# Top-k attention with a Fourier mix: the first batch's top-k mask computed on GpSimd alone

## Chip, cores and metric

The kernel runs on one core of a Trainium2 chip. The metric is the device time of one execution in microseconds (us). The engines are named as in the profile: PE (TensorE, matrix products and transposes) with PEld (its weight loads), DVE (VectorE), ACT (ScalarE), POOL (GpSimd) and SP (SyncE, which issues the DMAs).

## What is computed

The inputs are q, k and v of 8 batches, 8 heads, 576 tokens and 64 dimensions, and two weights of 512 x 2048 and 2048 x 512. Everything is float32 inside the kernel; the weights can come as float64 words and are then converted on the chip.

```python
scores = scale * np.matmul(q, k.transpose(0, 1, 3, 2))
kth = np.partition(scores, -32, axis=-1)[..., -32:-31]
scores = np.where(scores >= kth, scores, -1000000000.0)
scores = scores - np.max(scores, axis=-1, keepdims=True)
attn = np.exp(scores)
attn = attn / (np.sum(attn, axis=-1, keepdims=True) + 1e-09)
x = np.matmul(attn, v)               # then heads side by side: 8 x 576 x 512
mixed = np.real(np.fft.fft(np.fft.fft(x, axis=1), axis=2))
u = x + mixed
un = (u - mean(u)) / np.sqrt(var(u) + 1e-06)
out = u + np.maximum(un @ w_ch1, 0.0) @ w_ch2
```

Of each row of 576 scores, the 32 largest are kept and the rest are given a weight of zero by the exponential. The Fourier transforms are done as products with tables of cosines and sines.

## The kernel before

**Tiles and steps.** The attention is cut into 288 tiles of 128 rows and 576 scores (`items`): two heads at a time (a pair), nine tiles for each pair, four pairs and so 36 tiles (`PER_BATCH`) for each batch. One loop with the index `i` runs over the tiles, and one pass of it is a step. The order in which each engine gets its instructions is the order in which this loop emits them: the schedule is written out by hand, engines work through their queues in that order, and semaphores hold an instruction until its inputs are there. Some work is put into a plan with a step and a place in the step (`at(step, where, fn)`), and the loop fetches it there.

**What a tile needs.** `scores` multiplies on PE and copies the result on ACT into a buffer `S` in the on-chip memory (lines L335, L353, L364). `top_ops` finds the 32 largest values on DVE in four rounds: MAX8 (L382) gives the eight largest of a row, and MATCH_REPLACE8 (L384) takes them out in a work buffer `wk`. The four groups of eight are in `M8`. `bounds` (L391) multiplies the first and the last of these 32 by -1 and by the constant `FAR` (2^100) on POOL, into `nt`. `mask` then makes, on ACT, the value relu(-FAR * s + FAR * m32) in `wk` (L398), which is zero where the score is kept and huge elsewhere, and subtracts it on POOL from the score (L399). `expo` (L405) takes the exponential on ACT, and sums the row. `transposes` turns the result on PE (L426, L437, L441), ACT copies it out (L429, L438, L442, L444), and `attend` multiplies with v (L463). `to_tokens` transposes the outcome back (L503), and DVE divides by the sums (L490, L507, L514).

**First batch and later ones.** In the first batch the chain is short: in step i, `bounds(i)` and `mask(i)` are emitted at the end of the step, and `expo(i-1)` and `transposes(i-1)` in the middle of it. From tile 36 on, `mask(i-1)` is emitted one step later, and the transposes two steps later. In the first batch there is also the conversion of the weights, one block of 128 x 512 in nearly every step from step 1 to 33: three operations on ACT (L186, L202, L205) at the beginning of the step, one on DVE (L193), and two on POOL (L212 and L213) after the mask's subtraction. Two stages of matmuls with a matrix of equal entries (L1202) give the means of a part of the weights in steps 19 and 27, ACT copies these out (L1215), and POOL subtracts them (L1211) in eight of the first batch's steps; the other half follows after the first batch.

**After the first batch.** Once its 36 tiles are done, DVE folds the token axis and the channel axis of the result (L601, L564, L548 and the copies L552 and L560), POOL folds the few rows left over, PE does the transform over tokens (`yp`, L633) and over channels (`mp`, L681), DVE adds these to x and takes the statistics (L687, L709, L710), PE transposes (L746), and the first multiplications of the two-layer block begin (L831). From here on the matmuls of that block for one batch are spread in `units` over the attention of the next.

The buffers that matter: six for `S`, three pairs for `wk`, five for `M8`, six for `nt`.

Of the kernel before, what the change touches and what calls it, by code (L numbers as in the profile page):

```python
# [12 lines left out]
AF = mybir.ActivationFunctionType  # L13
ALU = mybir.AluOpType

TOPK = 32
NEG = -3.4028234e38
FAR = 2.0 ** 100
# [46 lines left out]
def kernel(  # L65
# [9 lines left out]
    nc = tc.nc  # L75
# [3 lines left out]
    scale = 1.0 / float(D) ** 0.5  # L79
# [57 lines left out]
    cc = const.tile([P, 2], F32, name="cc", tag="cc")  # L137
# [80 lines left out]
    nat, qT_of, kT_of, v_of, PT, Ssb, Wk, Wp, M8, Nt = ({} for _ in range(10))  # L218
# [76 lines left out]
    PER_BATCH = NPB * PER_PAIR  # L295
# [91 lines left out]
    def bounds(i):  # L387

        if i < N:
            Nt[i] = small.tile([P, 2], F32, name=f"nt_{i}", tag="nt", bufs=6)  # L390
            nc.gpsimd.tensor_tensor(  # L391
                out=Nt[i], in0=M8.pop(i)[:, 0:TOPK:TOPK - 1], in1=cc, op=ALU.mult
            )

    def mask(i):

        w = Wk[i]
        nc.scalar.activation(out=w, in_=Ssb[i], func=AF.Relu, scale=-FAR, bias=Nt[i][:, 1:2])  # L398
        nc.gpsimd.tensor_tensor(out=w, in0=Ssb.pop(i), in1=w, op=ALU.subtract)  # L399

    def expo(i):
# [834 lines left out]
    for o, place in ((B12, w2_12), (B21, w2_21)):  # L1236
        at(PER_BATCH + 14, "load2", lambda o=o, place=place: nc.sync.dma_start(
            out=scr[:, o], in_=place
# [106 lines left out]
    i, carry = 0, 0.0  # L1345
    while i < N + 4 or plan or queue or sums:
# [58 lines left out]
        for n, fn in enumerate(fixed):  # L1405
            cost += fn()
            if n == n_mask:
                if PER_BATCH <= i - 1 < N:
                    mask(i - 1)
                run(i, "act")  # L1410
                for fn in out_next:
                    fn()
                out_next.clear()
            if n == min(n_tr, len(fixed) - 1) and PER_BATCH <= i - 1 < N:
                expo(i - 1)

            got += some(max(room * (n + 1) / len(fixed) - got, 1.1 if fn in preps else 0.0))
# [29 lines left out]
        run(i, "pool0")  # L1447
        some_sums(max(2.1 - planned, 0.0))
        bounds(i)

        some_sums(1.3)
        if i < PER_BATCH:
            mask(i)
# [45 lines left out]
```

## Time and profile before

| | |
|---|---|
| time, median of 3 runs | 1915.32 us (1914.49 to 1915.92) |
| profiled execution: span from the first to the last instruction | 1910.9 us |
| profiled execution: its own time | not listed apart; the three runs lie 3.6 to 5.0 us above the span |
| PE busy | 1802.4 us (94% of the span) |
| DVE busy | 1584.9 us (83%) |
| ACT busy | 1208.4 us (63%) |
| POOL busy | 870.5 us (46%) |
| relu L398 on ACT | 288 times, 788 ns |
| mask subtraction L399 on POOL | 288 times, 1416 ns |
| bounds L391 on POOL | 288 times, 192 ns |
| exponential L405 on ACT | 288 times, 780 ns |
| MAX8 L382 on DVE | 1152 times, 743 to 749 ns |
| join of the weights, L212 and L213 on POOL | 32 times each, 1288 and 1290 ns |

Busy time is the time in which an engine works on an instruction. A line such as L398 is a line of the kernel, and all of its executions are one group. In the timeline, each row has the start in us from the beginning of the span, the duration in us, the engine, the line, the operation, output<-input with their shapes, and how many instructions are merged into the row; in brackets stands how long the engine was idle before, and what ended that. In a list of waits, "A <- B: t, n, m" says that the engine of A was idle before A until B ended, t us in all, n times, and m us the longest. The granted clock is the share of TensorE's full speed that it was given.

### The profile page before, as it was taken

Reading aid. Unit: us, or ns where it says so; the run is one execution under the profiler, and the core shown is the slowest. Engines: PE = TensorE matmul, PEld = TensorE weight load, DVE = VectorE, ACT = ScalarE, POOL = GpSimd, SP = SyncE. Lnnn points to the kernel's source line nnn. Section 1 sums busy time; section 2 is a strip of 40 time slices with the busy share of each in tenths; the row PEclk is TensorE's granted clock in tenths of the full one; section 3 lists DMA queues with packets and bytes.
Section 4 is the critical chain, followed back from the end, with each engine's and each line's share of the span. In section 5 each row is a group of like instructions: output and inputs, shape, how many; then the busy total and the mean of one; then the engine's idle time right before and its main releaser. Section 6 shows DMA issues by size and latency. Waiting matters only on the chain.

```text
span 1910.9 us, 28281 instructions
## 1 busy us (share of the span) xinstructions
PE 1802.4 (94%) x9008; PEld 1195.1 (63%) x9008; DVE 1584.9 (83%) x3277; ACT 1208.4 (63%) x3078; POOL 870.5 (46%) x1158
## 2 busy tenths in 40 slices
PE   6666699999999999999999999999999999999999
PEld 3344475474666756766567656667567656767678
DVE  8999989999999998989899898888899988872110
ACT  6878657676766767666676667666676667652110
POOL 4768643545635364345535454345534454241022
PEclk8777799999999999999999999999999999999999
DMA  5333001321104111140013101140013102030132
GB/s 164 105 96 107 20 13 45 93 66 25 47 11 129 29 28 44 42 121 19 20 47 101 53 16 53 42 114 23 22 47 101 49 20 58 23 102 6 50 100 79
DMA packets 184339, 111.34 MB, mean 58 GB/s; under 512 B 125952, under 2 KB 174208, under 8 KB 184192
## 3 DMA queue, kind: packets, MB, share of 16 engines
q1 hardware_dynamic: 183408, 109.33, 20.0%
q8 instruction: 72, 1.18, 0.3%
q14 instruction: 75, 0.61, 0.1%
q10 hardware_dynamic: 784, 0.21, 0.1%
HBM read 93.76 MB, written 15.73 MB: 57 GB/s over the span
## 4 chain that ended last, share of the span: by engine, by line
PE 80%; POOL 8%; ACT 4%; issue 3%; DVE 2%; DMA 1%; SPq 0%; POOLq 0%; ACTq 0%; DVEq 0%
PE hp L831 25%; PE cp L858 10%; PE o L463 8%; PE sp L361 6%; PE tpP L426 5%; PE cw L1028 5%; PE cv L1028 4%; PE yp L633 3%; PE mp L681 3%; POOL wk L399 3%; PE cp L897 3%; POOL w L213 2%; POOL w L212 2%; PE sp_t L331 2%; DVE m L382 1%
## 5 line engine op out<-in xcount | busy, mean ns | idle before, releaser
L399 POOL TENSOR_TENSOR wk<-S,wk 128x576 f32<-128x576 f32 x288 | 407.8, 1416 | 797.8 <-ACT wk L398 768.9
L382 DVE MAX8 m<-wk 128x8 f32<-128x576 f32 x864 | 623.3, 749 | 5.3
L831 PE MATMUL hp<-unT,w 128*128 128x256 f32 (+1 forms) x2048 | 536.7, 409 | 2.6 <-ACT unT L749 2.6
L831 PEld LDWEIGHTS hp<-unT,w 128*128 128x128 f32 x2048 | 372.7, 190 | 123.5 <-issue 23.8
L384 DVE MATCH_REPLACE8 wk<-m,wk 128x576 f32<-128x576 f32 x576 | 427.6, 742 | 0.0
L405 ACT ACTIVATE wk<-wk,nt 128x576 f32<-128x576 f32 x288 | 224.7, 780 | 68.1 <-POOL wk L399 64.1
L426 PE MATMUL tpP<-ident,wk 128*128 128x128 f32 x1152 | 185.8, 286 | 70.5 <-ACT wk L405 45.1
L429 ACT COPY PT<-tpP 128x512 f32<-128x512 f32 (+1 forms) x320 | 171.1, 546 | 113.5 <-PE tpP L426 111.1
L398 ACT ACTIVATE wk<-S,nt 128x576 f32<-128x576 f32 x288 | 226.9, 788 | 22.6 <-POOL nt L391 21.5
L858 PE MATMUL cp<-w,hT 128*128 128x512 f32 x512 | 240.6, 598 | 0.0
L426 PEld LDWEIGHTS tpP<-ident,wk 128*128 128x128 f32 x1152 | 142.6, 146 | 144.3 <-ACT wk L405 66.4
L835 ACT ACTIVATE hT<-hp 128x320 f32<-128x320 f32 (+1 forms) x256 | 104.8, 409 | 192.7 <-PE hp L831 190.4
L382 DVE MAX8 m<-S 128x8 f32<-128x576 f32 x288 | 214.0, 743 | 8.2 <-ACT S L335 8.2
L384 DVE MATCH_REPLACE8 wk<-m,S 128x576 f32<-128x576 f32 x288 | 213.6, 742 | 0.0
L463 PE MATMUL o<-PT,v 128*64 128x256 f32 (+3 forms) x1440 | 193.8, 412 | 1.4 <-ACT PT L429 1.4
L364 ACT COPY S<-sp 128x512 f32<-128x512 f32 (+1 forms) x264 | 141.7, 588 | 54.2 <-PE sp L361 54.1
L361 PE MATMUL sp<-kT,qT 64*128 64x512 f32 (+1 forms) x528 | 162.0, 672 | 4.2 <-ACT means L1215 3.3
L463 PEld LDWEIGHTS o<-PT,v 128*64 128x64 f32 x1440 | 111.3, 152 | 72.5 <-issue 16.2
L858 PEld LDWEIGHTS cp<-w,hT 128*128 128x128 f32 x512 | 88.8, 190 | 86.3 <-issue 86.2
L973 POOL TENSOR_TENSOR hT<-hT 128x512 f32<-128x512 f32 x64 | 81.3, 1274 | 100.4 <-ACT hT L835 88.7
L1028 PE MATMUL cw<-w,hT 128*128 128x256 f32 x448 | 106.4, 383 | 1.4 <-POOL nt L391 1.2
L1028 PEld LDWEIGHTS cw<-w,hT 128*128 128x128 f32 x448 | 81.5, 190 | 18.6 <-issue 5.2
(143 smaller groups left out, 2147.5 us busy)
## 6 DMA issues: line engine op xcount, KB each, us to landing
w<-w_parts SPq DMA_DIRECT2D x82, 512.0 KB, 4.3
space<-in_moe_w_ch_dram SPq DMA_DIRECT2D x32, 512.0 KB, 3.3
nat<-in_q_dram SPq DMA_DIRECT2D x128, 64.0 KB, 2.2
v<-in_v_dram SPq DMA_DIRECT2D x128, 64.0 KB, 2.2
out_dram<-x SPq DMA_DIRECT2D x32, 256.0 KB, 2.1
nat<-in_k_dram SPq DMA_DIRECT2D x124, 64.0 KB, 2.1
w_parts<-w_t SPq DMA_DIRECT2D x8, 512.0 KB, 2.9
w_s<-w_parts SPq DMA_DIRECT2D x8, 512.0 KB, 4.8
```

The lines of the kernel that those rows point to most:

```text
L361: nc.tensor.matmul(sp[r], lhsT=qT[hd, q_cols], rhs=kT[hd, :], start=True, stop=True)
L382: ops.append(lambda src=src, m8=m8: nc.vector.max(out=m8, in_=src))
L384: ops.append(lambda src=src, m8=m8: nc.vector.match_replace(w, m8, src, NEG))
L398: nc.scalar.activation(out=w, in_=Ssb[i], func=AF.Relu, scale=-FAR, bias=Nt[i][:, 1:2])
L399: nc.gpsimd.tensor_tensor(out=w, in0=Ssb.pop(i), in1=w, op=ALU.subtract)
L405: nc.scalar.activation(out=w, in_=w, func=AF.Exp, bias=Nt.pop(i)[:, 0:1], accum_out=den_t[pair % 3][:, c:c + 1],)
L426: nc.tensor.transpose(tp[:, c, :], p_sb[:, k0 + P * c:k0 + P * (c + 1)], ident)
L429: nc.scalar.copy(out=pt[:, NF * he:NF * (he + 1), col:col + w], in_=tp[:, :, o:o + w])
L463: nc.tensor.matmul(o[D * e:D * (e + 1), c0:c1], lhsT=vv[:, c, e, :], rhs=pt[:, 2 * NF if c == NF else NF * e + c, c0:c1], start=(c == 0), ...
L831: nc.tensor.matmul(hp[:, 0:w], lhsT=w1[:, dt, P * it:P * (it + 1)], rhs=unT[:, dt, 0:w], start=(dt == 0), stop=(dt == NDT - 1),)
L858: nc.tensor.matmul(cp, lhsT=hT[:, it, P * n:P * (n + 1)], rhs=w2[:, it, :], start=(it == 0), stop=(it == NIT - 1),)
L1028: nc.tensor.matmul(dst, lhsT=h()[a][:, kc, :], rhs=rhs_of(kc), start=start and kc == 0, stop=kc == NK - 1, skip_group_check=True,)
```

## The change

For the 36 tiles of the first batch, the mask's first half is done on POOL instead of ACT: one `tensor_scalar` compares each score with the 32nd maximum of its row (1 where it is less, 0 elsewhere) and multiplies by `FAR`. The subtraction on POOL stays as it was. `bounds` is still computed, since the exponential uses its first column; its second column isn't used in the first batch any more. `M8` is now released by the comparison and not by `bounds`. From tile 36 on nothing is changed.

```diff
         if i < N:
             Nt[i] = small.tile([P, 2], F32, name=f"nt_{i}", tag="nt", bufs=6)
+            m8 = M8[i] if i < PER_BATCH else M8.pop(i)
             nc.gpsimd.tensor_tensor(
-                out=Nt[i], in0=M8.pop(i)[:, 0:TOPK:TOPK - 1], in1=cc, op=ALU.mult
+                out=Nt[i], in0=m8[:, 0:TOPK:TOPK - 1], in1=cc, op=ALU.mult
             )
 
     def mask(i):
 
         w = Wk[i]
-        nc.scalar.activation(out=w, in_=Ssb[i], func=AF.Relu, scale=-FAR, bias=Nt[i][:, 1:2])
+        if i < PER_BATCH:
+            nc.gpsimd.tensor_scalar(
+                out=w, in0=Ssb[i], scalar1=M8.pop(i)[:, TOPK - 1:TOPK], scalar2=FAR,
+                op0=ALU.is_lt, op1=ALU.mult,
+            )
+        else:
+            nc.scalar.activation(
+                out=w, in_=Ssb[i], func=AF.Relu, scale=-FAR, bias=Nt[i][:, 1:2]
+            )
         nc.gpsimd.tensor_tensor(out=w, in0=Ssb.pop(i), in1=w, op=ALU.subtract)
```

## Prediction

> **What bounds the kernel now.** I read the table of busy time by stages first, then who waited for whom, then single steps in the timeline. In the first table the columns are length of the stretch, busy us and instructions of PE, PEld, DVE, ACT and POOL, granted clock, DMA share and GB/s:
>
> ```profile
> 16.00:130.00 114.00, 73.30 (x354) 46.76 (x353) 112.90 (x231) 93.30 (x217) 73.73 (x74) 0.78 0.38 121
> 130.00:220.00 90.00, 56.78 (x286) 36.38 (x286) 85.74 (x175) 71.82 (x168) 72.33 (x70) 0.74 0.25 75
> 262.00:1911.00 1649.00, 1624.37 (x8150) 1083.03 (x8148) 1341.59 (x2772) 1017.89 (x2628) 712.24 (x980) 1.00 0.19 53
> ```
>
> Two regimes are to be seen. From 262 us on PE is busy for 1624 of 1649 us, so whatever moves the moment at which PE enters that stretch moves the end by the same amount. Before it, in the 36 tiles of the first batch, DVE is the full engine (112.9 of 114 us; 85.7 of 90), with its top-32 search. The edit lies wholly in that first stretch, and takes work off ACT (93 of 114 us), which is not full. The waits up to 240 us (of DVE; sum, times, longest) and up to 280 us (of POOL) say who holds whom:
>
> ```profile
> DVE m L382 <- ACT S L335: 3.0, 5, 0.7
> DVE w L193 <- ACT wh L186: 0.7, 2, 0.4
> ```
>
> ```profile
> POOL wk L399 <- ACT wk L398: 63.9, 39, 5.2
> ```
>
> DVE hardly waits; what it does wait for is ACT's copies of later scores. POOL waits before nearly every mask subtraction for the relu on ACT. One undisturbed POOL round, from the timeline:
>
> ```profile
> 34.36 0.20 POOL L391 TENSOR_TENSOR nt<-m,cc 128x2 f32<-128x2 f32 x1
> 35.44 1.42 POOL L399 TENSOR_TENSOR wk<-S,wk 128x576 f32<-128x576 f32 x1 [0.89 <-ACT wk L398]
> 36.81 1.29 POOL L212 TENSOR_TENSOR w<-w,space 128x512 int32<-128x512 int32 x1
> 38.18 1.29 POOL L213 TENSOR_TENSOR w<-w,space 128x512 f32<-128x512 f32 x1
> 39.42 0.20 POOL L391 TENSOR_TENSOR nt<-m,cc 128x2 f32<-128x2 f32 x1
> ```
>
> A round is 5.06 us, 1.08 of them from the bounds to the subtraction with 0.89 idle. Eight rounds (tiles 20-23 and 28-31) also carry a weight centring (L1211) and take 6.28 us (140.58 to 146.86), while DVE's ordinary step is 5.55 us. So POOL, with ACT in its ring, falls behind: tile 20's maxima are ready at 129.2 and its bounds start at 133.55; for tile 32 the lag is 6.5 us. Behind POOL come ACT's exp and copies, and it is then that DVE runs dry: its idle times before 227 us are 0.44, 0.70, 0.70, 0.70, 0.56 and 0.34, together 3.44 us, all after 147 us. The last tile of the batch, 35:
>
> ```profile
> 219.99 0.19 POOL L391 TENSOR_TENSOR nt<-m,cc 128x2 f32<-128x2 f32 x1
> 223.31 0.80 ACT L398 ACTIVATE wk<-S,nt 128x576 f32<-128x576 f32 x1
> 224.19 1.41 POOL L399 TENSOR_TENSOR wk<-S,wk 128x576 f32<-128x576 f32 x1 [4.01 <-ACT wk L398]
> 225.63 0.78 ACT L405 ACTIVATE wk<-wk,nt 128x576 f32<-128x576 f32 x1 [1.52 <-POOL wk L399]
> 230.36 0.44 PE L503 MATMUL tpx<-ident,xT 128*128 128x128 f32 x2 [0.46 <-ACT xT L477]
> 231.00 0.17 DVE L490 RECIPROCAL rd<-rd 128x4 f32<-128x4 f32 x1
> 240.94 1.36 DVE L560 COPY fsp<-fsp 128x2 f32<-128x2 f32 x1
> 247.53 3.62 PE L681 MATMUL mp<-fd,y 128*128 128x256 f32 x16
> ```
>
> Its bounds are ready at 220.2, but ACT reaches the relu, behind its copies, only at 223.31. DVE's folds follow (to 242.3), the token DFT's second half runs 243.5 to 247.5, the channel DFT starts at 247.53, and PE's full stretch begins.
>
> **What the Trainium skill says.** The GPSIMD Engine Reference, section 4.1 Engine selection, calls one-input work on GpSimd roughly line rate and two-input work about twice as slow; its section 3.1 gives 1.03 cycles an element for a small body, about 1.8 for a good loop, about 2.6 with two inputs, and 12 with data-dependent branching. The trace agrees for two inputs: 128x576 in 1416 ns against 128x512 in 1274 ns is 2.2 ns an element. No wide one-input operation of POOL but a memset (128x513 in 520 ns) is in the trace. Perfetto Trace Analysis, section GPSIMD Engine Instruction, advises timing POOL by start-to-start spacing; I do so (1.24 us after an L213 shown as 1.29). SBUF — State Buffer, section Who interferes with whom, says that a DVE operation with two SBUF inputs, or in a two-port mode, and a GpSimd one block each other. One fold copy of DVE agrees: 1.24 us at 234.40 beside a mask subtraction, 0.17 at 239.53.
>
> **The change, part by part.** *Removed:* 36 relus of 0.78 us, 28 us of ACT, each of them a wait in ACT's queue for POOL's bounds, with the next step's three weight conversions (L186, L202, L205), exp and score copies queued behind it. ACT was not full, so the 28 us are worth only what they release. *Added:* 36 tensor_scalar operations of 128x576 on POOL, of a time T that the trace does not show. From below, a line-rate pass costs 0.19 (the shortest operations) + 576 x 0.82 ns (the memset's slope) = 0.66 us; the 1.8-cycle loop gives 0.19 + 0.86 = 1.05; as slow as the two-input form it would be 1.42; with branching, 5.9. I take 0.85, between the first two, as one input and two arithmetic steps. No DMA moves, and the last maxima's buffer is freed one instruction later, with five buffers: nothing.
>
> *POOL's round after.* Bounds to tensor_scalar 0.15 (the spacing after an L391), then T, 0.08 to a dependent operation (as from L212 to L213), then 3.98 as before: 4.22 + T, and 5.44 + T with centring. At T = 0.85 that is 5.07 and 6.29, what the unheld rounds are now. The work replaces the wait one for one; the gain is that holds longer than 0.89 us, 20 us in the 36 tiles, go. Tile 19 alone is held 5.2 us and starts the lag. Without that, tiles 20 to 32 cost POOL 8 x (5.44 + T) + 5 x (4.22 + T) = 64.6 + 13T, and DVE 77.7 - 2.5 of idle = 75.1: a lag at tile 33 of 13T - 10.5 = 0.6 us in place of 5.0.
>
> *What that is worth.* ACT and PE, no longer behind POOL, have the scores ready, and DVE's 3.44 us go. The folds then end at 242.3 - 3.4 = 238.9; PE, whose chain from tile 35 starts some 4 us earlier (subtraction about 1.1 us after the maxima, now 5.2), is waiting; the second half of the token DFT takes 4.0 us, and the channel DFT starts near 243.0 in place of 247.5: 4.5 us at most, apart from another 1 us if the fold copy is not blocked. If DVE keeps its waits, the same sum gives 246.4, a gain of 1.1. I take 4.3. The span goes from 1910.9 to 1906.6; about 4.4 us lie between the profiled span and the median of 1915.32, so the forecast is **1911.0**.
>
> **Rivals.** *Half of it, or nothing (0.22).* DVE's waits come from PE's long stages (the mean matmuls, 3.6 us in one piece, sit between scores and transposes) and not from POOL, or T is 1.1 to 1.45: between -3.5 and +3.5 us, near 1914. For it speaks that ACT's relu 19 waited not for POOL but for ACT's own queue behind those matmuls, which stay; against it, that every DVE wait falls in the stretch where POOL lags. That the relu's removal frees nothing because exp still needs POOL's subtraction belongs here.
>
> *POOL becomes the bound (0.28).* The mechanism is T alone, in POOL's queue from tile 20 on. The lag at tile 33 is 13T - 10.5; it changes by T - 1.45 to tile 34 (5.67 us of DVE) and by T - 4.26 to tile 35 (no joins), so tile 35's subtraction starts 16T - 16.0 us after its maxima, against 5.2 now. It decides from T = 1.33. At T = 1.65, with about 1 us carried from earlier tiles, that is +6 us: 1921.5. At 1.8, with 3.5 us carried, +11: 1926. Lateness here goes to the end undiminished, for DVE takes up tile 35's tokens at 231.00, 0.2 us after they are transposed. For it speaks that a comparison has to be turned into a number and multiplied, a longer body than any POOL runs here; against it, the single input.
>
> **How the numbers follow.** A difference within 0.2% (3.8 us) is about what a measurement of this kernel can tell from no change. The likeliest case straddles that line, 3.8 to 6 us faster with a chance of 0.50, its own range being 1909 to 1911.5; the middle case has 0.22, slower 0.28. The range runs from 1908.5 (all DVE waits and the blocked copy gone, and a little more) to 1922 (T about 1.65); left out are slower T, some 0.15, and a few hundredths below.
>
> **What would show it.** Right: tensor_scalar near 0.85 us; no L398 before 220 us; POOL's longest idle before L399 in tiles 1 to 35 near zero; tile 32's bounds within 3 us of its maxima; DVE without waits for S up to 227 us; the channel DFT starting near 243; PE's sum after it unchanged. Wrong: tensor_scalar above 1.3 us, with bounds ever further behind the maxima; or the waits of DVE for S still there with POOL on time, which would put them down to PE's stages.

## The result and the profile after

The changed kernel takes 1943.83 us (median of 4 runs, 1941.98 to 1947.8) against 1914.95 us of the kernel before (median of 4, those of the table and one more): 28.9 us slower, ratio 1.0151 with a 95% interval from 1.0137 to 1.0166. The profiled execution has a span of 1940.2 us, 29.3 more than before, and its own time is 1941.98, so 1.8 us lie around the span. The forecast of 1911.0 with a range to 1922 was wrong, and on the wrong side.

Busy time by stages of the kernel after, with the columns explained in the prediction:

```profile
16.00:130.00 114.00, 60.53 (x306) 38.89 (x306) 104.27 (x211) 71.27 (x172) 107.78 (x86) 0.70 0.37 115
130.00:220.00 90.00, 54.56 (x258) 32.95 (x258) 74.78 (x151) 56.12 (x135) 86.87 (x70) 0.73 0.25 76
300.00:1940.00 1640.00, 1614.65 (x8104) 1076.53 (x8102) 1334.26 (x2758) 1012.48 (x2616) 704.41 (x968) 1.00 0.19 54
```

POOL, the fifth engine, has gone from 73.7 to 107.8 us of 114 and from 72.3 to 86.9 of 90: it is now the full one. DVE has fallen from 112.9 to 104.3 and from 85.7 to 74.8. PE's long stretch is what it was, with 25 us idle. One POOL round in the timeline of the kernel after (L392 is the bounds, L400 the comparison, L408 the mask's subtraction):

```profile
41.55 0.20 POOL L392 TENSOR_TENSOR nt<-m,cc 128x2 f32<-128x2 f32 x1
41.83 2.21 POOL L400 TENSOR_SCALAR wk<-S,m 128x576 f32<-128x576 f32 x1
44.12 1.40 POOL L408 TENSOR_TENSOR wk<-S,wk 128x576 f32<-128x576 f32 x1
45.48 1.29 POOL L212 TENSOR_TENSOR w<-w,space 128x512 int32<-128x512 int32 x1
46.84 1.29 POOL L213 TENSOR_TENSOR w<-w,space 128x512 f32<-128x512 f32 x1
48.09 0.19 POOL L392 TENSOR_TENSOR nt<-m,cc 128x2 f32<-128x2 f32 x1
```

No row shows an idle bracket: POOL works without a pause, 6.54 us a round where the one of before took 5.06 with its wait. The comparison takes 2.21 us where 0.85 was assumed, and all 36 of them take 2.21 or 2.22. Who waits for POOL is seen in the list of waits of ACT from 16 to 255 us and of DVE to 255 us, kernel after:

```profile
ACT wk L414 <- POOL wk L408: 73.3, 32, 6.3
```

```profile
DVE m L382 <- ACT S L335: 28.7, 14, 4.1
DVE x L516 <- PE tpx L512: 1.3, 1, 1.3
DVE w L193 <- ACT wh L186: 0.7, 2, 0.5
```

ACT's exp (L414) waits for POOL's subtraction 32 times, 73.3 us in all. ACT's copies of later scores stand behind exp in its queue, and so DVE waits 28.7 us for scores where it waited 3.0. The longest of these waits, in the timeline:

```profile
228.27 0.78 ACT L414 ACTIVATE wk<-wk,nt 128x576 f32<-128x576 f32 x1 [3.27 <-POOL wk L408]
229.05 0.30 ACT L335 COPY S<-sp_t 128x64 f32<-128x64 f32 x2
229.34 0.76 DVE L382 MAX8 m<-S 128x8 f32<-128x576 f32 x1 [4.08 <-ACT S L335]
```

All three lines of DVE's list together are 30.7 us, against 3.7 before: 27.0 us more, and that is the loss but for 0.8 us at the channel transform. It passes unchanged through the rest: the channel transform of the first batch starts 27.8 us later (247.53 before), and so does that of the second batch.

```profile
275.29 3.62 PE L690 MATMUL mp<-fd,y 128*128 128x256 f32 x16
```

### The profile page after: what moved, and what is told of

It is laid out like the page before. It is cut to its first block, busy times and chain, and to the rows that moved or that the text cites. A ratio compares the mean times of both kernels' runs of the same rounds, so it can differ in the third digit from the quotient of the medians.

```text
span 1940.2 us, 28332 instructions
## 1 busy us (share of the span) xinstructions
PE 1800.9 (93%) x9008; PEld 1194.7 (62%) x9008; DVE 1584.5 (82%) x3277; ACT 1186.0 (61%) x3042; POOL 949.1 (49%) x1194
## 4 chain that ended last, share of the span: by engine, by line
PE 79%; POOL 7%; DVE 6%; ACT 4%; issue 2%; DMA 2%; SPq 0%; POOLq 0%; DVEq 0%; ACTq 0%
PE hp L840 25%; PE cp L867 10%; PE o L472 7%; PE sp L361 6%; PE tpP L435 5%; PE cw L1037 5%; PE cv L1037 4%; PE yp L642 3%; PE mp L690 3%; PE cp L906 3%; DVE m L382 3%; DVE wk L384 2%; POOL wk L400 2%; POOL wk L408 2%; PE sp_t L331 2%
## 5 line engine op out<-in xcount | busy, mean ns | idle before, releaser
L408 POOL TENSOR_TENSOR wk<-S,wk 128x576 f32<-128x576 f32 x288 | 406.9, 1413 | 749.8 <-ACT wk L405 717.9
L414 ACT ACTIVATE wk<-wk,nt 128x576 f32<-128x576 f32 x288 | 225.1, 781 | 135.4 <-POOL wk L408 131.3
L405 ACT ACTIVATE wk<-S,nt 128x576 f32<-128x576 f32 x252 | 198.9, 789 | 11.5 <-POOL nt L392 10.6
L1037 PEld LDWEIGHTS cw<-w,hT 128*128 128x128 f32 x448 | 81.5, 190 | 19.4 <-issue 5.2
```

What stands on the lines that cost most here:

```text
L414: nc.scalar.activation(out=w, in_=w, func=AF.Exp, bias=Nt.pop(i)[:, 0:1], accum_out=den_t[pair % 3][:, c:c + 1],)
L1037: nc.tensor.matmul(dst, lhsT=h()[a][:, kc, :], rhs=rhs_of(kc), start=start and kc == 0, stop=kc == NK - 1, skip_group_check=True,)
```

## The experiments

### Which part of the operation costs 2.2 us

The first batch's comparison was replaced by twelve forms in turn; this is the core of the edit:

```diff
-            nc.gpsimd.tensor_scalar(
-                out=w, in0=Ssb[i], scalar1=M8.pop(i)[:, TOPK - 1:TOPK], scalar2=FAR,
-                op0=ALU.is_lt, op1=ALU.mult,
-            )
+            form(i % 12, w, Ssb[i], M8.pop(i)[:, TOPK - 1:TOPK])
...
+        if n == 0:
+            ts(out=o, in0=s, scalar1=m32, scalar2=FAR, op0=ALU.is_lt, op1=ALU.mult)
...
+        elif n == 5:
+            ts(out=o, in0=s, scalar1=0.5, scalar2=1.0, op0=ALU.mult, op1=ALU.add)
+        elif n == 6:
+            ts(out=o, in0=s, scalar1=0.5, scalar2=None, op0=ALU.mult)
...
```

> The 36 masks of the first batch use twelve forms of the one-input operation on POOL in turn, three tiles each, all 128x576 (two forms as two halves of 288); the mask itself is therefore not computed in 33 of them. If the comparison is what is slow: forms with is_lt 2.2 us, forms with subtract, mult, add, min or max at most 1.1 us. If the second arithmetic step is: one-step forms about 1.1 us, two-step forms 2.2 us. If the per-partition scalar is: forms with it 2.2, with two immediates at most 1.1 us. If tensor_scalar on POOL as such is slow: all near 2.2 us, the copy alone near 0.7. If the time is per element and not per instruction, a half takes 1.2 us; if it is a fixed cost, a half takes over 1.8 us.

From the groups by line and shape of this kernel (after the bar: busy us in all, mean ns of one). L399 is is_lt and mult, L405 subtract and min, L401 is_lt alone, L411 mult alone with an immediate, L409 mult and add, L421 the copy, L415 and L419 the halves of L399 and L409:

```profile
L415 POOL TENSOR_SCALAR wk<-S,m 128x288 f32<-128x288 f32 x6 | 7.5, 1255 | 0.5
L405 POOL TENSOR_SCALAR wk<-S,m 128x576 f32<-128x576 f32 x3 | 6.7, 2223 | 0.0
L399 POOL TENSOR_SCALAR wk<-S,m 128x576 f32<-128x576 f32 x3 | 6.7, 2223 | 0.3
L401 POOL TENSOR_SCALAR wk<-S,m 128x576 f32<-128x576 f32 x3 | 5.2, 1733 | 0.0
L411 POOL TENSOR_SCALAR wk<-S 128x576 f32<-128x576 f32 x3 | 5.0, 1661 | 0.0
L419 POOL TENSOR_SCALAR wk<-S 128x288 f32<-128x288 f32 x6 | 2.5, 436 | 0.0
L409 POOL TENSOR_SCALAR wk<-S 128x576 f32<-128x576 f32 x3 | 2.0, 679 | 0.0
L421 POOL COPY wk<-S 128x576 f32<-128x576 f32 x3 | 2.0, 666 | 0.0
```

None of the four causes that were expected is right by itself. It isn't the comparison: subtract and min take as long, and a single multiplication takes 1.66 us, more than twice the pair of mult and add. That the time is per element, and not a fixed cost, came true: a half takes 1.26 us, and 576 columns against 288 give 3.4 ns an element for is_lt and mult, and 0.84 for mult and add. A second step costs 0.5 us in the dear forms, a scalar for each partition 0.08.

Twelve more forms were run to find where the cheap kind ends:

```diff
+        if n == 0:
+            ts(out=o, in0=s, scalar1=0.5, scalar2=0.5, op0=ALU.mult, op1=ALU.add)
...
+        elif n == 3:
+            ts(out=o, in0=s, scalar1=m32, scalar2=m32, op0=ALU.mult, op1=ALU.add)
+        elif n == 4:
+            ts(out=o, in0=s, scalar1=0.5, scalar2=m32, op0=ALU.mult, op1=ALU.subtract)
+        elif n == 5:
+            ts(out=o, in0=s, scalar1=0.5, scalar2=0.5, op0=ALU.add, op1=ALU.mult)
...
```

> Twelve more forms of the one-input operation of 128x576 on POOL, three tiles each in the first batch, whose mask is left out by that. If the fast time of 0.68 us belongs to mult followed by add: mult and add with a scalar for each partition, also 0.7 us; all others 1.65 to 2.25 us, also mult and mult, add and mult, max and min. If it belongs to two immediates without comparison: mult and mult, add and mult, max and min, subtract and mult with immediates 0.7 us, those with a partition's scalar 1.7 to 2.25 us.

The groups of this kernel: L399 is mult and add with immediates, L405 the same with two scalars for each partition, L411 mult and mult, L409 add and mult, L407 mult and subtract, L421 subtract and mult with immediates, L413 max and min:

```profile
L407 POOL TENSOR_SCALAR wk<-S,m 128x576 f32<-128x576 f32 x3 | 6.7, 2222 | 0.0
L421 POOL TENSOR_SCALAR wk<-S 128x576 f32<-128x576 f32 x3 | 6.4, 2147 | 0.0
L413 POOL TENSOR_SCALAR wk<-S 128x576 f32<-128x576 f32 x3 | 6.4, 2141 | 0.0
L405 POOL TENSOR_SCALAR wk<-S,m 128x576 f32<-128x576 f32 x3 | 2.5, 818 | 0.0
L399 POOL TENSOR_SCALAR wk<-S 128x576 f32<-128x576 f32 x3 | 2.0, 673 | 0.0
L411 POOL TENSOR_SCALAR wk<-S 128x576 f32<-128x576 f32 x3 | 2.0, 671 | 0.0
L409 POOL TENSOR_SCALAR wk<-S 128x576 f32<-128x576 f32 x3 | 2.0, 671 | 0.0
```

Neither expectation is right in full: the scalars for each partition are cheap with mult and add, as the first said, but mult and mult and add and mult are cheap as well, and max and min is not, against the second. In the 20 different forms tried, the cheap ones are exactly those of two steps that are both mult or add, 0.67 to 0.82 us whatever the operands (add followed by add was not tried). Every other one takes 1.65 to 2.22 us. The copy is cheap, too. Why the others are dear is not shown.

### Was the rest of the sum right? T turned to 0.68 and to 1.73 us

Two kernels differ from the changed one in the form alone:

```diff
-                out=w, in0=Ssb[i], scalar1=M8.pop(i)[:, TOPK - 1:TOPK], scalar2=FAR,
-                op0=ALU.is_lt, op1=ALU.mult,
+                out=w, in0=Ssb[i], scalar1=0.5, scalar2=1.0, op0=ALU.mult, op1=ALU.add
```

> As the changed kernel, but the one-input operation in the first batch is mult by 0.5 and add 1.0, the form that took 0.68 us; the mask of the first batch is left out by that, the work of all other instructions stays. Theory 1 (the step that failed was T alone, the rest of the prediction's sum holds): POOL's round is 5.0 us without and 6.2 us with centring, bounds start within 2 us of the maxima for tile 32, DVE's waits for scores before 227 us are gone, the channel DFT starts near 243 us, and the time is 3.5 to 5 us below before: ratio 0.9974 to 0.9982. Rival (DVE's waits come from PE's and ACT's long stages): POOL is on time and the waits stay; the gain is 1 us or less, ratio 0.9993 to 1.0003.

Measured: 1910.01 against 1914.9 us, ratio 0.9976 (0.9965 to 0.9987), 4.9 us faster. DVE's waits up to 230 us in this kernel are those of the first scores and of the start alone:

```profile
DVE S L335 <- PE sp_t L331: 8.1, 1, 8.1
DVE cc L1136 <- PEq L1488: 0.8, 1, 0.8
```

The channel transform starts 7.8 us earlier than before:

```profile
239.71 3.62 PE L690 MATMUL mp<-fd,y 128*128 128x256 f32 x16
```

Tile 32's bounds start 1.7 us after its maxima (6.5 before), and a round with centring takes 6.1 us. So POOL, freed of its wait for the relu, does take DVE's waits with it. With the mask left out, exp gets other values; it takes 0.78 us here, as in the kernels before and after.

```diff
-                out=w, in0=Ssb[i], scalar1=M8.pop(i)[:, TOPK - 1:TOPK], scalar2=FAR,
-                op0=ALU.is_lt, op1=ALU.mult,
+                out=w, in0=Ssb[i], scalar1=M8.pop(i)[:, TOPK - 1:TOPK], scalar2=None,
+                op0=ALU.is_lt,
```

> As the changed kernel, but with the comparison alone, without the multiplication by the constant: T is 1.73 us in place of 2.21, and the mask of the first batch is left out. Theory 1 (a queue with a threshold: only what POOL's round has above DVE's step of 5.66 us adds up): round 6.06 us, 0.40 above; the sum of the prediction gives 11.7 us behind the maxima at tile 35, some 4.2 carried from the tiles before 20 and 1.8 for the dearer start of the operation, less 5.2 now: 10 to 14 us slower than before, ratio 1.005 to 1.0075. Rival (the loss is in proportion to POOL's added work): 28.9 x 1.73 / 2.21 = 22.6 us slower, ratio 1.0118.

Measured: 1924.98 against 1914.9 us, ratio 1.0055 (1.0041 to 1.0069), 10.1 us slower, at the low end of what the queue with a threshold gives and less than half of what proportion would. Three points, at T = 0.68, 1.73 and 2.21, give -4.9, +10.1 and +28.9 us: from 1.73 to 2.21 the cost is 18.8 us for 36 x 0.48 = 17.3 us of added work, one for one within the intervals; from 0.68 to 1.73 it is 15.0 us for 37.8 us of work. Below the threshold added work goes into POOL's idle time, and above it everything counts. POOL's round in this kernel is 5.95 us (6.06 were expected). An estimate from such rounds says where the threshold lies: without the operation, POOL's 34 rounds from tile 1 to 35 are 148 us, and DVE's 34 steps without waits took 193 in the kernel with the fast form, so the two meet at T = 45 / 34 = 1.3 us. From there 34 times the excess is 14 us at T = 1.73 and 31 at 2.21; measured against the kernel with the fast form, it is 15.0 and 33.8.

### Was the relu's time on ACT worth anything?

First the relu was kept, and the comparison done beside it:

```diff
         nc.scalar.activation(out=w, in_=Ssb[i], func=AF.Relu, scale=-FAR, bias=Nt[i][:, 1:2])
+        m8 = M8.pop(i)
+        if i < PER_BATCH:
+            nc.gpsimd.tensor_scalar(
+                out=extra, in0=Ssb[i], scalar1=m8[:, TOPK - 1:TOPK], scalar2=FAR,
+                op0=ALU.is_lt, op1=ALU.mult,
+            )
         nc.gpsimd.tensor_tensor(out=w, in0=Ssb.pop(i), in1=w, op=ALU.subtract)
```

> ACT's relu stays and makes the mask; POOL does the comparison as well, for all 36 tiles, into a space that nobody reads. Theory 1, the loss is POOL's queue alone and the relu's 28 us on ACT were worth nothing: POOL's round is 6.5 us as in the changed kernel, and the time lies within 3 us of it, 1941 to 1947 us. Rival, the relief of ACT did bring a few us that POOL's queue then ate: 1949 us or more, since the relu is back and the comparison too. Rival, the loss comes from exp having to wait for one instruction more on its chain and not from POOL's total: under 1930 us, since here nothing waits for the comparison's result.

Measured: 1949.58 against 1914.5 us, ratio 1.0183 (1.0167 to 1.02). That is 35.1 us slower than before, 6 us more than the change. The second expectation holds by its number; the third, that the chain and not the total counts, falls. In this kernel POOL waits for the relu again, as its waits from 16 to 262 us say:

```profile
POOL wk L405 <- ACT wk L398: 7.2, 5, 3.4
```

The kernel after has no such wait in its first batch (one of 5.0 us comes later, at tile 36). The 7.2 us that a full POOL stands still are about the extra 6.8 us of span (1947.0 against 1940.2). Is it ACT's busy time, or is it that POOL waits for ACT? To part the two, the kernel with the fast form got a relu back that neither waits for POOL nor is waited for:

```diff
             M8.pop(i)
+            nc.scalar.activation(out=extra, in_=Ssb[i], func=AF.Relu, scale=-1.0, bias=cc[:, 1:2])
             nc.gpsimd.tensor_scalar(
```

> As the kernel with the fast form on POOL (mask of the first batch left out), but ACT does a relu of 128x576 at the old place all the same, into a space that nobody reads and with a constant bias, so that it waits for nothing of POOL's and POOL for nothing of it. Theory A (what the fast form gained came from taking POOL's subtraction out of ACT's queue): ratio to before 0.9972 to 0.9983, as without the relu. Theory B (it came from ACT's 0.7 us a step, which let ACT and PE catch up after the hole at tile 19): most of the gain goes, ratio 0.9988 to 1.0003.

Measured: 1909.02 against 1915.47 us, ratio 0.9967 (0.9955 to 0.9979), 6.4 us faster, a little more than theory A allowed; with the fast form alone it was 0.9976, and the intervals overlap. DVE's waits to 230 us are again only those of the start, and the channel transform starts 0.2 us later than with the fast form alone:

```profile
239.93 3.62 PE L691 MATMUL mp<-fd,y 128*128 128x256 f32 x16
```

So the 28 us of relu that ACT no longer did were worth next to nothing. What was worth 5 to 6 us is that POOL's subtraction no longer waited for the relu, or the relu for POOL's bounds; which of the two it was, the next section shows. Theory B falls.

### Ways to have that gain with the mask in place

Two tiles only, those before which POOL waited longest:

```diff
+ON_POOL = (19, 35)
...
-        if i < PER_BATCH:
+        if i in ON_POOL:
             nc.gpsimd.tensor_scalar(
```

> Only tiles 19 and 35, where POOL waited over 4 us for the relu in the kernel before, use the comparison on POOL; the other 34 keep the relu. Theory 1: the comparison with its start costs 2.6 us in place of 5.4 and 4.2, so tile 20 to 27 lag 2.8 us less, tile 35's subtraction starts 1.6 us earlier, one or more of DVE's waits of 0.7 us for scores disappear: 0.5 to 3 us faster than before, ratio 0.9985 to 0.9997. Rival, ACT's late relu is the end of its late step there and exp can't run earlier anyway: ratio 0.9997 to 1.0005.

Measured: 1913.9 against 1914.5 us, ratio 0.9994 (0.9985 to 1.0003). This decides nothing: the interval takes in both expectations.

Next, the relu's bias was made on ACT, so that only POOL still waits:

```diff
+        if i < PER_BATCH:
+            far = small.tile([P, 1], F32, name=f"far_{i}", tag="far", bufs=2)
+            nc.scalar.mul(out=far, in_=M8.pop(i)[:, TOPK - 1:TOPK], mul=FAR)
+            bias = far
```

> As the kernel before, with the relu on ACT, but in the first batch its bias (the 32nd maximum times the constant) is made by a small operation on ACT from the maxima, so that the relu waits no longer for POOL's bounds. Theory 1 (POOL's lag is what makes DVE run dry): the relu runs while POOL still joins weights, POOL's round shrinks to about 4.2 us without and 5.4 us with centring, DVE's waits for scores before 227 us go, and the time is 2.5 to 4.5 us below before: ratio 0.9976 to 0.9987. Rival (ACT and PE set DVE's waits, and ACT now has 36 x 0.2 = 7 us more): ratio 0.9995 to 1.003.

Measured: 1914.25 against 1914.9 us, ratio 0.999 (0.9982 to 0.9998), between the two expectations, with an interval that touches both. So to be rid of ACT's wait for POOL's bounds alone brings little. POOL's round with centring did shrink to 5.37 us (141.87 to 147.24), but POOL still waited for tile 19's relu until 129.65, tile 20's bounds started at 133.63 (133.55 before), and 5.4 us against DVE's 5.55 catches up hardly anything: for tile 32 the lag was still 5.0 us. The lag is made at tile 19, where ACT is late behind PE's mean matmuls, and POOL waits with it. In the kernel before, these (L1202) run for 3.67 us from 123.84, and a copy of scores that stands ahead of relu 19 in ACT's queue waits for PE behind them:

```profile
127.77 0.43 ACT L335 COPY S<-sp_t 64x64 f32<-64x64 f32 x2 [2.96 <-PE sp_t L331]
```

With the fast form, tile 20's bounds start at 129.32.

Then the order of POOL's own work was changed so that it has something to do while the relu runs ("low" is the first half of the join, L212):

```diff
         if i < PER_BATCH:
...
+            run(i, "shift")
+            run(i, "low")
             mask(i)
```

> As the kernel before, with the relu on ACT for all tiles; only POOL's order in a step is changed: bounds, first half of the weights' join (L212), mask subtraction, second half (L213), so that the first half covers the wait for the relu. If POOL's rounds with the relu's wait were the lag: POOL's round is about 4.3 us, DVE's waits shrink, ratio 0.9978 to 0.999. If ACT's and PE's own steps are the lag: exp is ready no earlier, ratio 0.999 to 1.001.

Measured: 1913.34 against 1915.47 us, ratio 0.9985 (0.9977 to 0.9993), 2.1 us faster: what the first theory expected. DVE's waits for scores up to 245 us fall from 3.0 to 1.3 us. With the comparison on POOL for tiles 19, 34 and 35 as well:

```diff
+ON_POOL = (19, 34, 35)
...
-        if i < PER_BATCH:
+        if i in ON_POOL:
             nc.gpsimd.tensor_scalar(
```

> The join split as in the kernel with the new order, and the comparison on POOL for tiles 19, 34 and 35 only, where ACT is late or POOL has no weights to join. Theory B: ACT loses three relus where it is latest, tile 35 comes 1 to 2 us earlier than with the split alone: 1 to 2 us below the split alone, ratio to before 0.997 to 0.9985. If tile 35 and the hole at tile 19 are bound by PE's mean matmuls: the same as the split alone within 0.0005.

Measured: 1911.79 us, ratio to before 0.9981 (0.9973 to 0.9989), 3.7 us faster than before; tile 35's subtraction starts at 218.75 in place of 224.19 (221.02 with the split alone). This version beats both kernels. That it beats the split alone isn't shown: 1.5 us lie between the medians, and the intervals overlap.

## Why the prediction was wrong

- **What bounds.** Right: DVE's search in the first batch, PE after it. PE's idle time after the first batch is the same within a us, and the 27.8 us arrive whole at the end.
- **The price T: the step that failed.** The value 0.85 was taken between a line-rate pass (0.66) and a good loop (1.05) "as one input and two arithmetic steps". It is 2.21 us. The line rate that the Trainium skill's GPSIMD Engine Reference gives for one input (section 4.1, Engine selection) is true in these runs for the copy, and for pairs of mult and add, but not for a comparison, a minimum, a subtraction or even one multiplication: is_lt and mult cost 3.4 ns an element against 2.2 for the two-input subtraction. The truth lay between two of the prices named (1.42 and 5.9), above what the range took in, and nothing of before shows such an operation.
- **The rounds.** 4.22 + T with T = 2.21 gives 6.43; 6.54 was measured, for the comparison starts 0.28 us after the bounds and not 0.15.
- **The rival "POOL becomes the bound".** The mechanism, the engine and the sign were right, with 0.28 for a chance. Its own sum, from tile 20 on, falls short: at T = 2.21 the lag of tile 35 would be 16T - 16.0 = 19.4 us, 14 more than before, half of the loss. Counted from tile 1, the rounds give all of it: 24 rounds of 6.54 us, 8 with centring of 7.77 and 2 without a join of 3.93 are 227 us, which is what POOL took (21.89 to 249.04), and before it took 198 (21.97 to 219.99): 29 us. So its place was wrong: with rounds of 6.54 against the 5.67 us of DVE's average step without waits the queue falls behind from the second tile on, and lateness doesn't pile up to tile 35, whose subtraction starts 5.1 us after its maxima, about as before (5.3). It is paid on the way, in DVE's waits for scores.
- **The gain side.** The sum (4.3 us faster at T = 0.85) is near the 4.9 us at T = 0.68, and its reason holds: no waits of DVE for scores. (They were 3.7 us before and not 3.44; one of 0.23 at 201.93 was left out.) That the number fits so well is luck in part, for two terms were off and nearly cancelled. The channel transform starts at 239.7, not 243.0: DVE takes up tile 35's tokens 4.6 us earlier (226.41 against 231.00), its folds take 1.1 us less, and PE, which began the second half of the token transform 1.2 us after they were done, begins it 1.0 us before that. Of these 7.8 us, 3.3 are given back until the second batch's transform (488.37 against 492.85), which the last section takes up, and the spans of the two profiled executions differ by 2.7 us.
- **The rival "half of it".** Its argument, that ACT is late by PE's mean matmuls and not by POOL, is what makes the lag at tile 19; but with POOL's wait for ACT gone, there is no lag at tile 20 (bounds at 129.32, maxima at 129.2).
- **Around the span.** The 4.4 us set between span and median were too much: 1.8 us lie around the span in the executions whose own time is known. By that the profiled execution of before took some 1912.7 us (an estimate), less than any of the four runs of the result.

## What to carry to other kernels

A one-input operation isn't cheap on POOL because it has one input: measure the pair of operations itself, and first see whether it can be written in two steps of mult and add. The mask needs a comparison, a maximum or a minimum, and no form with one of these was cheap. An engine that waits in every round has room for work up to its wait and little more: here that room ended at about T = 1.3 us, and what came above it was paid in every tile. What a wait on another engine costs is not the time of that engine's work; that POOL no longer waited for ACT was worth 5 to 6 us, while ACT's own 28 us were worth next to nothing.

## What the runs showed of the hardware

tensor_scalar of POOL has two speeds, 0.84 and some 3.4 ns an element for two steps, and one step alone is among the dear ones (1.66 us for mult, 0.68 for mult and add, 128x576). And in the kernel with the fast form, the clock granted to TensorE, which is 1.00 after the first batch in the profile of before, drops twice more. The stretch ahead of each drop and the first drop itself, from the table of stages (columns as in the first table of the prediction; the second drop, from 474.14, looks like the first):

```profile
337.61:341.02 3.41, 1.14 (x4) 0.25 (x2) 3.38 (x8) 3.11 (x13) 3.41 (x5) 1.00 0.38 84
341.02:344.43 3.41, 3.41 (x14) 1.79 (x15) 3.34 (x6) 2.29 (x6) 1.00 (x3) 0.50 0.67 233
470.73:474.14 3.41, 1.43 (x10) 0.90 (x12) 3.34 (x8) 3.33 (x11) 1.73 (x3) 1.00 0.00 0
```

Each drop is 3.41 us at half the clock, so both together cost 3.4 us of full clock, about the 3.3 us given back between the first and the second batch's transform. The kernel with the relu that nobody reads has one such drop, from 253.20, and gives back 1.7 us in the same stretch. The Trainium skill (TensorE: Matmul & The Clock Gate, Part 1: The HAM clock gate) says that the clock is halved after a window of about 3.4 us, not bound to the kernel's start, in which PE was idle. The traces agree on the window: in each of eleven, all but that of the two tiles, the changes of the clock lie on a grid of 3.413 us (474.14 - 341.02 is 39 of them), which starts at another place in each. They do not agree on how idle PE must be. Cut along this grid, the eleven traces have five windows between the end of the first batch and 1890 us in which PE was busy for 1.14 to 1.43 us, and each of these is followed by one at half clock (the two above, the one before 253.20, and one each in the kernels with the comparison alone and with the second twelve forms). In every other window PE was busy for 1.56 us or more, and none of these is followed by a drop. So an idle time of 2.1 to 2.3 us, which the kernel before has as well, brings a drop when most of it falls into one window, and none when it is divided between two. That is read from these traces; no run moved the grid on purpose.
